# Loading w3 in two awaited halves, and running the last matmuls in four column tiles with four evacuating copies

## Chip, cores, metric

The kernel runs on 1 core of a Trainium2 chip. The metric is the time of one execution on the device, in microseconds, taken as the median of several runs. A profile is one execution; its span (193.5 us for the kernel before) is counted from the first to the last instruction and is about 1.8 us shorter than the time. All times in profiles below are counted from the span's start.

## The reference, cut to what matters

One decode step of a small transformer block for 8 sequences: a layernorm, attention over a window of 2048 cached keys and values (64 MB of K and V), and then an MLP part. Only the end matters here:

```python
h = x + attention(layernorm(x)) @ wo                 # [8, 512]
# with one token the shifted branch through w1, w2 is zero, so
# B(y) = y + gelu(layernorm(y) @ w3) @ w4, y = layernorm(h)
out = h + B(layernorm(h))                            # w3 [512, 1792], w4 [1792, 512], bf16
```

## The kernel before

All loads go through one DMA queue, in one order; the weights of the last stages come last:

```python
order += [("wo", 0), ("wo", 1), ("w3", 0), ("w4", 0)]
...
elif kind == "w3":
    e.dma_start(w3_sb, B_w3.rearrange("(k p) f -> p k f", k=KC)).then_inc(sem_w3, 16)     # 1792 KB
else:                                        # w4 in three pieces: 1024, 512 and 256 KB
    ...                                      # W4_CUT = [0, 8, 12, 14], of FC = 14 row chunks
    e.dma_start(w4_dst[:, c0:c1, :], w4_rows[:, c0:c1, :]).then_inc(sem_w4[i], 16)
```

The end of the compute, cut. `uT` is the normalized input, transposed; `hpx_hi`, `hpx_lo` are the residual in two bf16 parts. In `pe_fin` the 8 columns of a chunk of `gT` are the stationary operand and w4 streams; with NQ = 2 the output columns 0 to 255 go to PSUM partitions 0 to 7 and columns 256 to 511 to partitions 32 to 39, that is to two column tiles of the array.

```python
NQ = 2
DQ = D // NQ
def pe_h3(e):                                # L757: 14 x 4 matmuls of 8 columns
    e.wait_ge(sem_w3, 16)
    e.wait_ge(sem_dveP, DVEP_U)
    for fc in range(FC):
        for kc in range(KC): ...             # w3 chunk stationary, uT moving
def act_gelu(e): ...                         # L768: gT <- misc
def pe_fin(e):
    ...                                      # L778: residual, 8 matmuls of 128 columns
    e.wait_ge(sem_actP, ACTP_G)
    for fc in range(FC):                     # L787
        if fc in W4_CUT:
            e.wait_ge(sem_w4[W4_CUT.index(fc)], 16)
        for j in range(NQ):
            ins = e.matmul(fin_ps[32 * j:32 * j + B, :], gT[:, fc * B:(fc + 1) * B],
                           w4_sb[:, fc, j * DQ:(j + 1) * DQ], ..., tile_position=(0, 32 * j))
def dve_final(e):                            # L797
    e.tensor_copy(out_sb[:, 0:DQ], fin_ps[0:B, :])
def act_final(e):                            # L804
    e.activation(out_sb[:, DQ:D], fin_ps[32:32 + B, :], ACT.Copy)
```

Of the kernel before, what the change touches and what calls it, by code (L numbers as in the profile page):

```python
# [7 lines left out]
ACT = mybir.ActivationFunctionType  # L8
# [3 lines left out]
B = 8  # L12
D = 512
# [8 lines left out]
FC = F // 128  # L22
KC = D // 128
# [14 lines left out]
def bass_sequential_preLN__sliding_block_cached__mixer_s_mlp__decode_kernel(  # L38
# [24 lines left out]
    with es:  # L63
        sb = lambda shape, dtype, name: es.enter_context(nc.sbuf_tensor(name, shape, dtype))
        ps_t = lambda shape, dtype, name: es.enter_context(nc.psum_tensor(name, shape, dtype))
        S = lambda name: es.enter_context(nc.semaphore(name))
# [62 lines left out]
        hpx_lo = sb([128, KB], dt.bfloat16, "hpx_lo")  # L129
        uT = sb([128, KB], dt.bfloat16, "uT")  # L130
        gT = sb([128, FC * B], dt.bfloat16, "gT")
        NQ = 2
        DQ = D // NQ
        out_sb = xln_b

# [4 lines left out]
        misc = ps_t([128, 512], dt.float32, "misc")  # L140
# [3 lines left out]
        H3 = slice(384, 384 + FC * B)  # L144
# [1 line left out]
        sem_slot = [S(f"sem_slot{i}") for i in range(NS)]  # L146
        sem_x = S("sem_x")
        sem_wq = S("sem_wq")
        sem_w3 = S("sem_w3")
        sem_w4 = [S(f"sem_w4_{i}") for i in range(3)]  # L150
        sem_wo = [S(f"sem_wo{i}") for i in range(4)]
        sem_out = S("sem_out")
# [27 lines left out]
        sem_dveP = S("sem_dveP")  # L180
        sem_actP = S("sem_actP")
# [53 lines left out]
        w3_sb = slots[:, place[("w3", 0)][0], 0:KC * F].rearrange("p (k f) -> p k f", k=KC)  # L235
# [11 lines left out]
        def sp_prog(e):  # L247
            e.dma_start(wq_sb, A_wq.rearrange("(p k) n -> p (k n)", k=KC)).then_inc(sem_wq, 16)  # L248

            def free_slot(n):  # L250
                if n >= NS:
                    kind, t = order[n - NS]
                    if kind == "k":
                        e.wait_ge(sem_Thi, NT * (t + 1))
                    else:
                        e.wait_ge(sem_PV, t + 1)
                elif n >= NS - 2:
                    e.wait_ge(sem_dveP, DVEP_QBLK)

            for n, (kind, t) in enumerate(order):  # L260
                free_slot(n)
                slot = n % NS
                dst = slots[:, slot, :]
                if kind in "kv":
                    b, gq = divmod(t, 2)
                    cache = A_k_cache if kind == "k" else A_v_cache
                    src = cache[b, GL * gq:GL * (gq + 1), W0:SK, :].rearrange("g (p c) d -> p g (c d)", c=C)
                    e.dma_start(dst, src).then_inc(sem_slot[slot], 16)  # L268
                elif kind == "wo":
                    for i in range(len(WO_CUT) - 1):  # L270
                        h0, h1 = WO_CUT[i], WO_CUT[i + 1]
                        if h0 // WO_HALF == t:
                            f0 = (h0 % WO_HALF) * D
                            e.dma_start(dst[:, f0:f0 + (h1 - h0) * D],
                                        A_wo.rearrange("(p j) n -> p (j n)", j=NJ)[:, h0 * D:h1 * D]).then_inc(sem_wo[i], 16)
                elif kind == "w3":
                    e.dma_start(w3_sb, B_w3.rearrange("(k p) f -> p k f", k=KC)).then_inc(sem_w3, 16)
                else:
                    w4_rows = B_w4.rearrange("(c p j) n -> p c (j n)", p=128, j=2)
                    w4_dst = w4_sb.rearrange("p (c j) n -> p c (j n)", j=2)  # L280
                    for i in range(len(W4_CUT) - 1):
                        c0, c1 = W4_CUT[i] // 2, W4_CUT[i + 1] // 2
                        e.dma_start(w4_dst[:, c0:c1, :], w4_rows[:, c0:c1, :]).then_inc(sem_w4[i], 16)
            e.wait_ge(sem_dveP, DVEP_OUT_READY)
            e.wait_ge(sem_actP, ACTP_OUT_READY)
            e.dma_start(out.rearrange("b s d -> (b s) d"), out_sb[:, :]).then_inc(sem_out, 16)
            e.wait_ge(sem_out, 16)
# [386 lines left out]
        fin_ps = b6[:, 0:DQ]  # L674
# [73 lines left out]
        PEP_H3 = ev_pe.next()  # L748

        def pe_h3(e):  # L750
            e.wait_ge(sem_w3, 16)
            e.wait_ge(sem_dveP, DVEP_U)
            ins = None
            for fc in range(FC):
                c, j = divmod(fc, 2)
                for kc in range(KC):
                    ins = e.matmul(misc[:, H3.start + fc * B:H3.start + (fc + 1) * B],  # L757
                                   w3_sb[:, kc, c * 256:(c + 1) * 256].rearrange("p (q j) -> p j q", j=2)[:, j, :],
                                   uT[:, kc * B:(kc + 1) * B],
                                   start=(kc == 0), stop=(kc == KC - 1))  # L760
            ins.then_inc(sem_peP, 1)
        PE.append(pe_h3)

        ACTP_G = ev_act.next()
# [8 lines left out]
        def pe_fin(e):  # L773
            e.wait_ge(sem_dveP, DVEP_RES)
            for half in (hpx_hi, hpx_lo):
                for k in range(KC):
                    j, kk = divmod(k, KC // NQ)
                    e.matmul(fin_ps[32 * j:32 * j + B, kk * 128:(kk + 1) * 128], half[:, k * B:(k + 1) * B],  # L778
# [4 lines left out]
# [5 lines that stand above are left out]
# [6 lines left out]

        def dve_final(e):
            e.wait_ge(sem_peP, PEP_FIN)
            e.tensor_copy(out_sb[:, 0:DQ], fin_ps[0:B, :]).then_inc(sem_dveP, 1)  # L797
        DV.append(dve_final)

        ACTP_OUT_READY = ev_act.next()  # L800

        def act_final(e):
            e.wait_ge(sem_peP, PEP_FIN)
            e.activation(out_sb[:, DQ:D], fin_ps[32:32 + B, :], ACT.Copy).then_inc(sem_actP, 1)  # L804
        AC.append(act_final)

        with nc.Block() as block:
            block.gpsimd(pool_prog)
            block.sync(sp_prog)

            @block.tensor
            def _(e):
                for f in PE:
                    f(e)

            @block.scalar
            def _(e):
                for f in AC:
                    f(e)

            @block.vector
            def _(e):
                for f in DV:
                    f(e)
# [28 lines left out]
```

## Time and profile before

| what | before |
|---|---|
| time, median (range) | 195.37 us (195.1 to 195.4, 3 runs) |
| DMA engines busy, slices 2 to 38 of 40 | 9 tenths or more |
| HBM read | 79.18 MB, 409 GB/s over the span |
| w3 / first piece of w4 lands (all of it has arrived) | 185.6 / 188.2 us |
| last matmul ends | 191.3 us |
| output DMA issued, span ends | 191.8, 193.5 us |

The page's activity rows, two of them (busy tenths in 40 equal slices of the span; the granted clock of TensorE in tenths of full speed):

```profile
PEclk9999999859999999699999998899999999998557
DMA  6999999999999999999999999999999999999981
```

The DMA row is full until the last two slices: the kernel is bound by its loads, and only what comes behind the last loads can be shortened. The next fence is the end of the chain of waits, in order of time (start, length, what):

```profile
150.91 37.24 DMA slots<-in_B_w_dram
188.16 0.14 issue
188.29 3.03 PE b L787 x28
191.32 0.02 issue
191.34 0.41 DVE xln_b L797
```

From 150.91 to 188.16 us everything that ended last was waiting for a load of B's weights, here the first piece of w4; then 28 matmuls, then one copy on VectorE beside one on ScalarE. The timeline of the same stretch shows what stood ready and what did not (start, length, engine, line, operation, count; in brackets the idle time before it and what ended that):

```profile
184.31 0.19 DVE L734 SCALAR_TENSOR_TENSOR uT<-hm,r 128x32 bf16<-128x32 f32 x1
185.66 1.66 PE L757 MATMUL misc<-uT,slots 128*128 128x8 bf16 x56 [2.62 <-DMA slots<-in_B_w_dram]
187.35 0.26 ACT L768 ACTIVATE gT<-misc 128x112 bf16<-128x112 f32 x1 [1.61 <-PE misc L757]
188.29 3.01 PE L787 MATMUL b<-slots,gT 128*8 128x256 bf16 x28 [0.45 <-DMA slots<-in_B_w_dram]
191.34 0.37 ACT L804 ACTIVATE xln_b<-b 8x256 bf16<-8x256 f32 x1 [3.73 <-PE b L787]
191.34 0.41 DVE L797 CAST xln_b<-b 8x256 bf16<-8x256 f32 x1 [5.84 <-PE b L787]
```

uT was ready at 184.50 and the w3 matmuls waited for w3 until 185.66. That looks like lost time. But the gelu ended at 187.61, and the last matmuls still had to wait for w4, until 188.29: the w3 stage had 0.55 us to spare. The windows of this stretch (start:end, length, busy us of PE, PEld, DVE, ACT, POOL with counts, granted clock, DMA share, GB/s) show two more things:

```profile
186.00:186.50 0.50, 0.50 (x25) 0.50 (x22) 0.00 (x0) 0.00 (x0) 0.00 (x0) 0.50 1.02 397
187.00:187.50 0.50, 0.50 (x18) 0.48 (x17) 0.00 (x0) 0.15 (x1) 0.00 (x0) 0.50 0.59 225
189.00:189.50 0.50, 0.50 (x8) 0.29 (x6) 0.00 (x0) 0.00 (x0) 0.00 (x0) 0.50 0.58 201
191.00:191.50 0.50, 0.30 (x6) 0.00 (x0) 0.15 (x1) 0.16 (x1) 0.00 (x0) 0.97 0.00 0
```

The clock stands at half in the whole tail (in the trace of before it rises at 191.03, and the last two matmuls took 280 and 277 ns in place of 417). And from about 186.7 us on the DMA share falls to 0.59.

### The profile page before, as it was taken

The page shows a single profiled execution, that of the slowest core. Times are in us where ns is not written, and L with a number is a line of the kernel's source. Part 1 is how long each engine was busy: PE and PEld are TensorE (multiplying, and loading weights), DVE is VectorE, ACT ScalarE, POOL GpSimd, SP SyncE. Part 2 cuts the span into 40 slices and gives each one's busy share as a digit, 9 for nine tenths or more (in the row PEclk, how much of TensorE's full clock was granted, in tenths as well). Part 3 has the DMA queues.
Part 4 walks back from the last instruction along what each step waited for, and adds up shares of the span by engine and source line. Part 5 has one row for each costly group of instructions (what it writes and reads, how often), then busy time and mean ns, then how long its engine had stood idle before and what let it go on. Part 6 is the DMA issues. An engine that isn't in the chain of part 4 may idle for free.

```text
span 193.5 us, 4989 instructions
## 1 busy us (share of the span) xinstructions
PE 152.7 (79%) x2088; PEld 106.2 (55%) x2088; DVE 106.4 (55%) x277; ACT 90.3 (47%) x109; POOL 4.7 (2%) x14
## 2 busy tenths in 40 slices
PE   2037999399979993999799766999699999765555
PEld 0037878286647562766475444756566684435443
DVE  7811447343787375447763672558647877673220
ACT  3110577924494465245944382348445965400040
POOL 8000000000000000000000000000000000000000
PEclk9999999859999999699999998899999999998557
DMA  6999999999999999999999999999999999999981
GB/s 225 427 433 433 427 430 430 430 425 433 430 433 423 425 427 433 433 423 433 427 433 422 427 427 430 433 423 433 433 427 427 430 435 427 433 422 402 412 331 40
DMA packets 6853, 79.50 MB, mean 411 GB/s; under 512 B 672, under 2 KB 688, under 8 KB 2352
## 3 DMA queue, kind: packets, MB, share of 16 engines
q1 hardware_dynamic: 6816, 79.18, 96.6%
q8 instruction: 17, 0.28, 0.5%
q14 instruction: 4, 0.03, 0.0%
q10 hardware_dynamic: 16, 0.01, 0.0%
HBM read 79.18 MB, written 0.01 MB: 409 GB/s over the span
## 4 chain that ended last, share of the span: by engine, by line
DMA 80%; PE 17%; SPq 1%; issue 0%; DVE 0%
DMA slots<-in_A_k_cache_dram 60%; DMA slots<-in_B_w_dram 19%; PE kT_ps L430 9%; PE S_ps L462 2%; PE misc L551 2%; PE b L787 2%; PE b L551 2%; SPq L268 1%; PE misc L513 0%; PE misc L573 0%; DVE xln_b L797 0%; SPq L248 0%; PE b L573 0%
## 5 line engine op out<-in xcount | busy, mean ns | idle before, releaser
L441 ACT ACTIVATE kT_sb<-kT_ps 128x1024 bf16<-128x1024 bf16 x64 | 65.3, 1023 | 68.9 <-PE kT_ps L430 68.9
L430 PE MATMUL kT_ps<-perm_b,slots 128*128 128x128 bf16 x1024 | 72.2, 228 | 17.4 <-DMA slots<-in_A_k_cache_dram 17.0
L430 PEld LDWEIGHTS kT_ps<-perm_b,slots 128*128 128x128 bf16 x1024 | 62.4, 103 | 34.9 <-DMA slots<-in_A_k_cache_dram 20.5
L447 DVE COPY kT_sb<-kT_ps 128x1024 bf16<-128x1024 bf16 x64 | 43.7, 685 | 54.0 <-PE kT_ps L430 53.9
L462 PE MATMUL S_ps<-kT_sb,qstrip 128*32 128x512 bf16 x256 | 24.8, 399 | 0.3 <-DVE kT_sb L447 0.3
L496 ACT ACTIVATE P_sb<-S_ps,mtile 128x1024 bf16<-128x1024 f32 x16 | 17.8, 1113 | 2.4 <-DVE mtile L485 2.4
L551 PE MATMUL misc<-slots,pT_sb 128*64 128x512 bf16 x128 | 16.7, 384 | 1.1 <-DVE mrl L519 1.1
L551 PE MATMUL b<-slots,pT_sb 128*64 128x512 bf16 x128 | 16.5, 384 | 0.0
L530 DVE TENSOR_TENSOR pT_sb<-kT_ps,maskT 128x1024 bf16<-128x1024 bf16 x16 | 10.6, 688 | 2.8 <-PE kT_ps L430 2.5
L430 PE MATMUL kT_ps<-ident_b,P_sb 128*128 128x128 bf16 x128 | 11.0, 254 | 0.0
L430 PEld LDWEIGHTS kT_ps<-ident_b,P_sb 128*128 128x128 bf16 x128 | 9.4, 116 | 2.3 <-issue 1.5
L551 PEld LDWEIGHTS misc<-slots,pT_sb 128*64 128x64 bf16 x128 | 6.1, 109 | 7.9 <-issue 3.0
L462 PEld LDWEIGHTS S_ps<-kT_sb,qstrip 128*32 128x32 bf16 x256 | 5.9, 93 | 6.8 <-ACT kT_sb L441 0.8
L551 PEld LDWEIGHTS b<-slots,pT_sb 128*64 128x64 bf16 x128 | 6.1, 109 | 6.1 <-issue 1.5
L567 DVE SCALAR_TENSOR_TENSOR o_sum<-b,mrl,o_sum 128x128 f32<-128x128 f32 x24 | 8.4, 351 | 0.8
L567 DVE SCALAR_TENSOR_TENSOR o_sum<-misc,mrl,o_sum 128x128 f32<-128x128 f32 x24 | 8.4, 350 | 0.8
L679 ACT ACTIVATE std<-var,eps_t 128x8 f32<-128x8 f32 x1 | 0.3, 300 | 17.1 <-DVE var L730 17.1
L363 PE MATMUL b<-ident_b,xln_b 8*128 8x8 bf16 x4 | 0.3, 174 | 7.9 <-DVE xln_b L340 7.9
L474 DVE TENSOR_REDUCE mtile<-S_ps 128x1 f32<-128x512 f32 x8 | 5.4, 681 | 0.6 <-PE S_ps L462 0.6
L363 PEld LDWEIGHTS b<-ident_b,xln_b 8*128 8x128 bf16 x4 | 0.2, 114 | 8.8 <-DVE xln_b L340 8.8
L383 PE MATMUL S_ps<-xlnT,slots 128*128 128x8 bf16 x128 | 3.6, 168 | 1.6 <-DMA slots<-in_A_wq_dram 1.6
L697 PE MATMUL S_ps<-opl,slots 128*128 128x8 bf16 x128 | 4.0, 168 | 0.8 <-DMA slots<-in_A_wo_dram 0.8
(96 smaller groups left out, 92.8 us busy)
## 6 DMA issues: line engine op xcount, KB each, us to landing
slots<-in_A_k_cache_dram SPq DMA_DIRECT2D x16, 2048.0 KB, 40.4
slots<-in_A_v_cache_dram SPq DMA_DIRECT2D x16, 2048.0 KB, 38.6
slots<-in_A_wq_dram SPq DMA_DIRECT2D x1, 4096.0 KB, 12.3
slots<-in_A_wo_dram SPq DMA_DIRECT2D x1, 2048.0 KB, 41.0
slots<-in_B_w_dram SPq DMA_DIRECT2D x1, 1792.0 KB, 39.5
slots<-in_A_wo_dram SPq DMA_DIRECT2D x1, 1024.0 KB, 34.0
slots<-in_A_wo_dram SPq DMA_DIRECT2D x2, 512.0 KB, 35.2
slots<-in_B_w_dram SPq DMA_DIRECT2D x1, 1024.0 KB, 37.2
```

The lines of the kernel that those rows point to most:

```text
L383: ins = e.matmul(S_ps[:, 0, h * B:(h + 1) * B], wq_v[:, kc, h * DH:(h + 1) * DH], xlnT[:, kc * B:(kc + 1) * B], start=(kc == 0), stop=(kc ...
L430: ins = e.matmul(kT_ps[n % 2][:, c * 128:(c + 1) * 128], src[:, c * 128:(c + 1) * 128], unit[:, :], is_transpose=True)
L441: e.activation(kT_sb[:, i % NKT, 0:W // 2], kT_ps[step_of[("k", i)] % 2][:, 0:W // 2], ACT.Copy).then_inc(sem_Elo, 1)
L447: e.tensor_copy(kT_sb[:, i % NKT, W // 2:W], kT_ps[step_of[("k", i)] % 2][:, W // 2:W]).then_inc(sem_Ehi, 1)
L462: ins = e.matmul(S_ps[32 * gl:32 * (gl + 1), b % 2, :], qstrip[:, b, GL * gq + gl, o:o + 32], kv[:, gl, :, :], start=(gq == 0 and qi == 0) ...
L474: ins = e.tensor_reduce(mtile[:, 2, 0:1], S_ps[:, j, :], AX.X, ALU.max)
L496: e.activation(P_sb[:, half * W // 2:(half + 1) * W // 2].rearrange("r (k g) -> r k g", g=GL), s_rep, ACT.Exp, bias=mtile[:, j, 0:1], scal ...
L530: e.tensor_tensor(pT_sb[:, :, half * hc:(half + 1) * hc, :].rearrange("p a c (g x) -> p (c g) a x", g=GL), kT_ps[n % 2][:, half * W // 2:( ...
L551: ins = e.matmul(pv_ps[gq][64 * a:64 * (a + 1), :].rearrange("p (q d) -> p q d", d=DH), pT_sb[:, gq, cc, :], vq[:, cc, :, :], start=(cc < ...
L567: ins = e.scalar_tensor_tensor(o_sum[:, gq, :], pv_ps[gq][:, q * DH:(q + 1) * DH], w[:, q:q + 1], o_sum[:, gq, :], ALU.mult, ALU.add)
L697: ins = e.matmul(hT_ps[:, k * B:(k + 1) * B], wo_at(h)[:, k * 128:(k + 1) * 128], opl[:, h, :], start=False, stop=(h == NJ - 1), skip_grou ...
L787: ins = e.matmul(fin_ps[32 * j:32 * j + B, :], gT[:, fc * B:(fc + 1) * B], w4_sb[:, fc, j * DQ:(j + 1) * DQ], start=False, stop=(fc == FC ...
```

## The change

Its intent: start the w3 matmuls as soon as the first half of w3 is there, and halve the time of the last matmuls by running four column tiles of 128 output columns side by side in place of two of 256. The evacuation, which is the copying of the result out of PSUM, then takes two copies on each engine. NQ = 4 also spreads the 8 residual matmuls over four tiles. In the w3 matmuls the first pass leaves all 14 sums open until the second pass adds the other two chunks of rows, and the `start` flag now stands on the very first matmul alone.

```diff
-        NQ = 2
+        NQ = 4
-        sem_w3 = S("sem_w3")
+        sem_w3 = [S(f"sem_w3_{i}") for i in range(2)]
...
-                    e.dma_start(w3_sb, B_w3.rearrange("(k p) f -> p k f", k=KC)).then_inc(sem_w3, 16)
+                    for i in range(2):
+                        k0, k1 = i * KC // 2, (i + 1) * KC // 2
+                        e.dma_start(w3_sb[:, k0:k1, :],
+                                    B_w3.rearrange("(k p) f -> p k f", k=KC)[:, k0:k1, :]).then_inc(sem_w3[i], 16)
...
-            e.wait_ge(sem_w3, 16)
             e.wait_ge(sem_dveP, DVEP_U)
-            for fc in range(FC):
-                for kc in range(KC): ...
-                                   start=(kc == 0), stop=(kc == KC - 1))
+            for half in range(2):
+                e.wait_ge(sem_w3[half], 16)
+                for fc in range(FC):
+                    for kc in range(half * KC // 2, (half + 1) * KC // 2): ...
+                                       start=(kc == 0 and fc == 0), stop=(kc == KC - 1), skip_group_check=True)
...
-            e.tensor_copy(out_sb[:, 0:DQ], fin_ps[0:B, :]).then_inc(sem_dveP, 1)
+            for j in range(NQ // 2):
+                ins = e.tensor_copy(out_sb[:, j * DQ:(j + 1) * DQ], fin_ps[32 * j:32 * j + B, :])
+            ins.then_inc(sem_dveP, 1)
...                                                                # and the same on ScalarE for j = 2, 3
```

More of the change, by code (lines that the diff above doesn't have):

```diff
@@ L750, in pe_h3 @@
         def pe_h3(e):
-            e.wait_ge(sem_w3, 16)
             e.wait_ge(sem_dveP, DVEP_U)
             ins = None
-            for fc in range(FC):
-                c, j = divmod(fc, 2)
-                for kc in range(KC):
-                    ins = e.matmul(misc[:, H3.start + fc * B:H3.start + (fc + 1) * B],
-                                   w3_sb[:, kc, c * 256:(c + 1) * 256].rearrange("p (q j) -> p j q", j=2)[:, j, :],
-                                   uT[:, kc * B:(kc + 1) * B],
-                                   start=(kc == 0), stop=(kc == KC - 1))
+            for half in range(2):
+                e.wait_ge(sem_w3[half], 16)
+                for fc in range(FC):
+                    c, j = divmod(fc, 2)
+                    for kc in range(half * KC // 2, (half + 1) * KC // 2):
+                        ins = e.matmul(misc[:, H3.start + fc * B:H3.start + (fc + 1) * B],
+                                       w3_sb[:, kc, c * 256:(c + 1) * 256].rearrange("p (q j) -> p j q", j=2)[:, j, :],
+                                       uT[:, kc * B:(kc + 1) * B],
+                                       start=(kc == 0 and fc == 0), stop=(kc == KC - 1), skip_group_check=True)
             ins.then_inc(sem_peP, 1)
@@ L803, in act_final @@
             e.wait_ge(sem_peP, PEP_FIN)
-            e.activation(out_sb[:, DQ:D], fin_ps[32:32 + B, :], ACT.Copy).then_inc(sem_actP, 1)
+            for j in range(NQ // 2, NQ):
+                ins = e.activation(out_sb[:, j * DQ:(j + 1) * DQ], fin_ps[32 * j:32 * j + B, :], ACT.Copy)
+            ins.then_inc(sem_actP, 1)
         AC.append(act_final)
```

## The prediction

> **What bounds the kernel now.** DMA: the activity rows show the DMA engines at 9 tenths or more from slice 2 to slice 37, and the chain of waits gives 80% of the 193.5 us span to DMA. So only what follows the last weights can be saved. The chain in order of time ends: B weights in flight until 188.16 us; the 28 last matmuls 188.29 to 191.32; the evacuation 191.34 to 191.75; the output DMA to 193.5.
>
> The last landings, from the DMA issues with their times to landing: w3 issued 146.1 + 39.5 = 185.6; w4 in three pieces 150.9 + 37.2 = 188.1, 167.9 + 21.5 = 189.4, 177.5 + 12.5 = 190.0. The w3 matmuls run 185.66 to 187.2 (56 starts about 28 ns apart), the gelu ends at 187.61, and then PE waits, for w4 piece 0.
>
> **Half A, w3 in two halves.** The first half should land about 2.1 us before the second (896 KB at the 390 to 430 GB/s of these windows), near 183.4. uT is ready at 184.50 (timeline), so 28 matmuls run at about 184.6 to 185.4, the other 28 from 185.65 to about 186.4. The gelu then ends near 186.9 instead of 187.6. But w4 piece 0 lands only at 188.16, and the gelu already had 0.55 us of slack before it. I expect these 0.7 us to become wait: worth 0 by itself.
>
> **Half B, four column tiles.** The 28 matmuls of 256 columns start in pairs, 6 ns apart, a pair every 0.2135 us, at a granted clock of 0.50 (windows, 188 to 191). The Trainium skill ("TensorE: Matmul & The Clock Gate", back-to-back issue gap) gives N / 1.2 ns for a cold array: 213 for 256 columns, which this trace agrees with; two column tiles therefore already run side by side. With four tiles of 128 columns it gives 107 ns per group of four; the residual matmuls here (128 columns) follow each other in one tile every 106 ns. 56 weight loads and matmuls at the 28 ns per pair of the w3 stage give about the same: 14 groups x 107 to 112 ns = 1.5 to 1.6 us in place of 3.0.
>
> Not all of that is kept, because w4 pieces 1 and 2 now become waits: piece 0's eight groups 188.3 to 189.2, wait until 189.4; four groups to 189.95; wait until 190.05; two groups and the drain, end near 190.65. Before: 191.30. PE gain about 0.65 us.
>
> **Evacuation.** ACT took 374 ns and DVE 413 ns for 8x256, side by side. Now each makes two copies of 128. A DVE cast of 128 columns takes 279 ns here; two, overlapped, I estimate at 0.47 us, so 0.05 to 0.1 us more. The output DMA keeps its 1.75 us.
>
> **Sum.** -0.65 + 0.08 = about -0.6 us: 194.8 us, 8 in 10 between 194.2 and 195.3. Faster by over 2%: 0.01; within 2%: 0.97; slower: 0.02.
>
> **What would show it.** The wait of the w3 matmuls split in two, the second ending near 185.6; the gelu near 186.9 and a wait of over 1 us for w4 after it; last matmuls starting in fours about 0.11 us apart, with gaps near 189.3 and 190.0; last matmul end near 190.6, after which two copies per engine take about 0.47 us.
>
> **What would make it wrong.** The split w3 or the added instructions shifting the w4 landings (a few tenths of a us either way, the same size as the gain); groups of four not overlapping (56 x 107 ns = 6 us, 3 us slower); copies that do not overlap (+0.15 us); a clock that stays low does not matter much[...].

## The result, and the profile after

The changed kernel took 194.88 us (194.62 to 194.94, 4 runs) beside 195.38 us for the kernel before (195.1 to 195.61, 4 runs). A ratio is the mean time of one kernel's runs over that of the other's runs of the same rounds, so it is not quite the ratio of the medians: 0.998, 95% interval 0.9964 to 0.9995. It is 0.5 us less by the medians. In five more rounds (below) it was 0.68 us less, ratio 0.9964 (0.9951 to 0.9976). The prediction of 194.8 us, 194.2 to 195.3, holds. All outputs are right.

The timeline after, the lines that answer to those of before:

```profile
184.47 0.91 PE L761 MATMUL misc<-uT,slots 128*128 128x8 bf16 x28 [1.52 <-DVE uT L737]
185.60 0.91 PE L761 MATMUL misc<-uT,slots 128*128 128x8 bf16 x28 [0.22 <-DMA slots<-in_B_w_dram]
186.55 0.26 ACT L772 ACTIVATE gT<-misc 128x112 bf16<-128x112 f32 x1 [0.89 <-PE misc L761]
188.19 1.03 PE L791 MATMUL b<-slots,gT 128*8 128x128 bf16 x32 [1.37 <-DMA slots<-in_B_w_dram]
190.47 0.56 ACT L811 ACTIVATE xln_b<-b 8x128 bf16<-8x128 f32 x2 [3.65 <-PE b L791]
190.47 0.57 DVE L802 CAST xln_b<-b 8x128 bf16<-8x128 f32 x2 [5.05 <-PE b L791]
191.11 0.37 SPq L289 DMA_DIRECT2D out_dram<-xln_b  x1
```

The first half of the w3 matmuls now starts with uT, the gelu ends 0.8 us earlier (186.81), and all of that becomes a wait: PE sits idle 1.37 us, until the first piece of w4. The last matmuls come in three runs, 32, 16 and 8, and the chain of waits shows why:

```profile
167.88 21.47 DMA slots<-in_B_w_dram
189.35 0.04 issue
189.39 0.60 PE b L791 x16
189.99 0.04 issue
190.03 0.41 PE b L791 x8
190.44 0.02 issue
190.47 0.28 DVE xln_b L802
190.74 0.30 DVEq L815
```

The long wait now ends at 189.35, with w4's second piece, no longer with its first; the third lands at 189.98. The last matmul ends at 190.41, in place of 191.30, 0.89 us earlier. The evacuation (from the first copy's start to the output DMA's issue) takes 0.64 us in place of 0.46. The output DMA is issued at 191.11 in place of 191.81: 0.70 us earlier, and 0.70 us is also what the span lost (193.54 to 192.84). Each of these is one execution against one. The clock rise in the trace of before flatters before by about 0.14 us: from e1 to e2 below, which have no such rise before the matmuls end, the last matmul's end moves from 191.53 to 190.53, 1.0 us, and the output DMA's issue 0.80 us.

### The profile page after: what moved, and what is told of

Same layout as the page of the kernel before. It is cut to its first block, busy times and chain, and to the rows that moved or that the text cites. A ratio compares the mean times of both kernels' runs of the same rounds, so it can differ in the third digit from the quotient of the medians. Undisturbed runs are those within 1.5% of the kernel's fastest.

```text
span 192.8 us, 5048 instructions
## 1 busy us (share of the span) xinstructions
PE 151.7 (79%) x2116; PEld 105.5 (55%) x2116; DVE 106.4 (55%) x278; ACT 90.6 (47%) x110; POOL 4.8 (2%) x14
## 4 chain that ended last, share of the span: by engine, by line
DMA 76%; PE 18%; SPq 4%; DVE 1%; issue 0%; DVEq 0%
DMA slots<-in_A_k_cache_dram 65%; DMA slots<-in_B_w_dram 11%; PE kT_ps L433 10%; PE S_ps L465 2%; PE misc L554 2%; SPq L268 2%; PE b L554 2%; SPq L286 2%; PE b L791 1%; DVE kT_sb L450 0%; PE misc L516 0%; PE b L576 0%; PE misc L576 0%; SPq L248 0%; DVEq L815 0%
## 5 line engine op out<-in xcount | busy, mean ns | idle before, releaser
L576 PE MATMUL b<-o_sum,hsel 128*16 128x128 f32 x16 | 3.8, 330 | 1.4 <-DVE o_sum L570 1.4
```

The costliest lines, as they stand in the source:

```text
L576: e.matmul(pv_ps[v % 2][0:GL * R, OT], hsel[:, :], o_sum[:, v % 2, :], start=True, stop=True).then_inc(sem_oTm, 1)
```

## The experiments

Four theories were to be told apart. Mine: the landing of w4 sets the tail, so the w3 halves are worth nothing, and the tiles are worth only the part that does not turn into waits for w4's second and third pieces. The rivals: the halves do part of the work; the tiles cannot be fed faster than they were; and, for the two copies that took 0.57 us where I had expected 0.47, either a cost of changing the PSUM rows or plain lack of overlap.

### Each half of the change alone

e1: the changed kernel with

```diff
-        NQ = 4
+        NQ = 2
```

> The change's first half alone (w3 in two halves, two column tiles as before). Theory (the w4 landing near 188.1 us decides): 0 us; 195.4 +- 0.1; gelu ends near 186.8 instead of 187.6, then PE waits over 1.2 us for w4; last matmul still ends near 191.3. Rival (the halves give part of the gain): 0.2 to 0.5 us less, last matmuls starting earlier than 188.2.

Measured: 195.54 us beside 195.56, ratio 1.0001 (0.9987 to 1.0014). The timeline of e1:

```profile
186.78 0.26 ACT L772 ACTIVATE gT<-misc 128x112 bf16<-128x112 f32 x1 [1.20 <-PE misc L761]
188.38 3.15 PE L791 MATMUL b<-slots,gT 128*8 128x256 bf16 x28 [1.11 <-DMA slots<-in_B_w_dram]
```

The gelu ended at 187.04, the matmuls still waited for w4 until 188.38 and ended at 191.53. The halves alone are worth nothing, although they do exactly what they were meant to do.

e2: the kernel before with NQ = 4 and the four copies; w3 loaded and awaited whole:

```diff
-        NQ = 2
+        NQ = 4
-            e.tensor_copy(out_sb[:, 0:DQ], fin_ps[0:B, :]).then_inc(sem_dveP, 1)
+            for j in range(NQ // 2): ...          # as in the change; the same on ScalarE
```

> The change's second half alone (four column tiles and four copies, w3 as one load). Theory: the whole gain, 194.9 +- 0.15, last matmul ends near 190.4, copies as in the changed kernel. Rival: clearly slower than the changed kernel of the same rounds (by 0.2 us or more).

The timeline of e2:

```profile
188.35 2.17 PE L787 MATMUL b<-slots,gT 128*8 128x128 bf16 x56 [0.59 <-DMA slots<-in_B_w_dram]
```

e3: the changed kernel once more, no edit.

> The changed kernel once more, in the same rounds, to size the gain more tightly: the traces' shift of the output DMA's issue (191.81 to 191.11) says 0.7 us, the first timed runs say 0.5; between 194.6 and 195.0.

| run, same rounds | median us | ratio to before | 95% interval |
|---|---|---|---|
| before | 195.56 | | |
| e1, w3 halves alone | 195.54 | 1.0001 | 0.9987 to 1.0014 |
| e2, tiles and copies alone | 194.73 | 0.9960 | 0.9947 to 0.9972 |
| e3, the whole change | 194.88 | 0.9964 | 0.9951 to 0.9976 |

The tiles alone give all of the gain, 0.83 us here (194.82 beside 195.49 in a later set, r2 below: 0.67 us); the whole change gave 0.68. The intervals of e2 and e3 overlap. The first half of the change can be left out.

### The landing order turned round

If the halves and the tiles are worth more than they show because w4 lands last, then both must show their full worth when w3 lands last. That takes one edit, made to four kernels:

```diff
-        order += [("wo", 0), ("wo", 1), ("w3", 0), ("w4", 0)]
+        order += [("wo", 0), ("wo", 1), ("w4", 0), ("w3", 0)]
```

f1 is the kernel before with it, f2 is e1 with it, f3 is e2 with it, f4 the changed kernel with it.

> The kernel before with w4 loaded ahead of w3, so that w3 is what lands last (near 190.1 us) and no wait for w4 remains behind it. It is the base for the three runs beside it. Chain after the landing: w3 matmuls 1.66, gelu 0.3, last matmuls 3.1, evacuation 0.41: about 3.8 us above the kernel before, 199.4.

> The same with w3 in two halves. Theory (the halves do shorten the path to the gelu, and were worth nothing only because w4 landed later): 0.7 to 0.8 us below the base run. Rival (halves give nothing by themselves, e.g. because the second load's landing or the split loop costs as much): within 0.2 us of the base run.

> The same base with four column tiles and four copies. Theory (about 0.5 us of the tiles' gain went into waits for w4 pieces 1 and 2): last matmuls of 1.5 + 0.3 us without a gap in place of 3.1, copies 0.16 us longer, so 1.1 to 1.3 us below the base run, against 0.7 to 0.8 in the real order. Rival (groups of four cannot be fed faster than they were): 0.7 to 0.8 us here too.

> Both halves of the change in this order. Theory: the two gains add, 1.8 to 2.1 us below the base run. Rival: no more than the tiles alone.

| run, same rounds | median us | against f1 | the same part in the real order |
|---|---|---|---|
| f1, before | 199.25 | | |
| f2, w3 halves | 198.56 | -0.69 | -0.02 (e1) |
| f3, tiles and copies | 197.97 | -1.28 | -0.83 (e2), -0.67 (r2) |
| f4, both | 197.17 | -2.08 | -0.68 (e3) |

Lines of the chain of waits of f1, then of f2, then of f3:

```profile
190.12 1.65 PE misc L757 x56
192.30 3.00 PE b L787 x28
```

```profile
190.07 0.91 PE misc L761 x28
191.50 3.00 PE b L791 x28
```

```profile
190.10 1.66 PE misc L757 x56
192.11 1.69 PE b L787 x56
```

And one line of the timeline of f3:

```profile
192.11 1.67 PE L787 MATMUL b<-slots,gT 128*8 128x128 bf16 x56
```

With nothing left to wait for, the 56 narrow matmuls run without a gap in 1.67 us from the first start to the last end, where the 28 wide ones took 3.16 (192.13 to 195.29 in the timeline of f1; the chain counts only the last 3.00 of it). In e2, with the waits for w4's second and third pieces, the same 56 took 2.17: 0.50 us more. The Trainium skill, "TensorE: Matmul & The Clock Gate", section "Back-to-back issue gap", gives N / 1.2 ns as the gap between single matmuls on a cold array. That is 107 ns for 128 columns, taken here as an estimate for a step of four tiles side by side; the trace of the changed kernel agrees, with 0.107 us from group to group of four at a granted clock of 0.50, after a first step of 0.06 (its 32 matmuls: 0.06 + 6 x 0.107 + 0.31 for the last one's own length = 1.01 of the 1.03 us shown). What sets the step is not told apart: the w3 matmuls follow each other every 27 ns, and four times that is 107 ns too. The halves, worth nothing before, are worth 0.69 us here. The two add up: 0.69 + 1.28 = 1.97, measured 2.08. So the rivals fall: neither part of the change is idle by itself, and the tiles can be fed. What they lost in the real order is the difference, about 0.5 us of the tiles' gain and all of the halves', and the wait that took it is the one for w4. The order itself is a bad one for this kernel (f1 is 3.6 us slower than the kernel before, 195.64 in these rounds), since more work stands behind the last landing.

### The two copies that did not overlap

I had expected two copies of 128 columns to take 0.47 us. In the changed kernel VectorE's second copy began 14 ns after the first had ended, ScalarE's 12 ns. The Trainium skill, "VectorE: DVE Perf Modes", section "Two Vector instructions with no wait between them", has a rule for that: an instruction whose input starts in another group of 32 partitions than the last instruction's input from the same memory is held until all earlier ones have finished. With four tiles the copies of one engine read PSUM rows 0 and 32 (VectorE) or 64 and 96 (ScalarE). e4 makes the same number of copies of the same size, but in the kernel before, where both copies of an engine read the same rows:

```diff
-            e.tensor_copy(out_sb[:, 0:DQ], fin_ps[0:B, :]).then_inc(sem_dveP, 1)
+            for j in range(2):
+                ins = e.tensor_copy(out_sb[:, j * 128:(j + 1) * 128], fin_ps[0:B, j * 128:(j + 1) * 128])
+            ins.then_inc(sem_dveP, 1)
...                                                # and the same on ScalarE, rows 32 to 39
```

> The kernel before with only its evacuation cut into four copies of 128 columns, so both copies of an engine read the same 32-row group of PSUM. Theory (the second copy in the changed kernel is held because its input starts in another 32-row group than the one before it): here DVE's two copies overlap, second start 60 to 150 ns before the first's end, pair about 0.45 us. Rival (two copies never overlap here, e.g. because both engines read one bank): gap of 10 to 15 ns and a pair of 0.56 us as in the changed kernel. Time 195.4 to 195.6.

Measured: 195.63 us beside 195.56 (ratio 0.9999, 0.9985 to 1.0013). The timeline of e4:

```profile
191.60 0.43 ACT L807 ACTIVATE xln_b<-b 8x128 bf16<-8x128 f32 x2 [3.88 <-PE b L787]
191.60 0.48 DVE L798 CAST xln_b<-b 8x128 bf16<-8x128 f32 x2 [5.96 <-PE b L787]
```

The pairs take 0.48 and 0.43 us in place of 0.57 and 0.56, with copies of nearly the same length in both kernels (278 and 269 ns on VectorE against 278 and 282 ns after; 268 and 253 ns on ScalarE against 270 and 273 ns). VectorE's second copy starts 70 ns before the first ends, ScalarE's 92 ns. So the change of PSUM rows, not the number of copies, takes the overlap away, as the page says for VectorE. (The columns read differ too: 0 to 127 in both copies of the changed kernel, 0 to 127 and 128 to 255 in e4. That was not separated.) It costs about 0.1 us on each engine here. The second copy by itself costs only about 0.07 us (0.48 against 0.41).

### An attempt at something better

Since the slowest DMA engines set the end, and the DMA share is 0.59 from 186.7 us on, I tried to find the engines that finish early and to give them more of w4. The Trainium skill, "DMA: Bandwidth & Descriptors", section "Why a DMA increments its semaphore by 16 and not by 1", says that a load is split over the largest k of at most 16 engines that divides its rows, on the lowest-numbered ones. So I put eight tiny loads of 14, 12, ... 1 rows ahead of w4 in e2:

```diff
+                    for n_, rows in enumerate((14, 12, 10, 8, 6, 4, 2, 1)):
+                        e.dma_start(dst[0:rows, FC * D + 128 * n_:FC * D + 128 * n_ + 98 + 2 * rows],
+                                    B_w1[0:rows, 0:98 + 2 * rows]).then_inc(sem_junk, 16)
```

Its first build asked for more SBUF than was left and did not build; the second used unused bytes of w4's slot.

> The tiles-alone kernel with eight tiny loads (14, 12, 10, 8, 6, 4, 2 and 1 rows of an unused input, each of its own size) put ahead of w4, to see in the packet times which of the 16 DMA engines are ahead when the last weights come. From 186.5 us on the DMA share is 0.59, so six or seven engines have finished some 3 us before the others. If the engines that are ahead are those that take the small loads (the first ones), the markers' packets start about 2.5 us before the others' and the last piece of w4 can be moved to them; if they are spread, nothing simple is to be had. Time not of interest, 194.7 to 195.5.

> The tiles-alone kernel with eight tiny loads (14, 12, 10, 8, 6, 4, 2 and 1 rows of an unused input, each of its own size, into unused bytes) put ahead of w4, to see in the packet times which of the 16 DMA engines are ahead when the last weights come. From 186.5 us on the DMA share is 0.59, so six or seven engines have finished some 3 us before the others. If the engines that are ahead are those that take the small loads (the first ones), the markers' packets start about 2.5 us before the others' and the last piece of w4 can be moved to them; if they are spread, nothing simple is to be had. Time not of interest, 194.7 to 195.8.

It is one run (195.17 us beside 195.48, state unknown), used for its packet times alone. The starts of the packets of the 14-, 2- and 1-row loads, read from the packed trace since no view lists single packets, in us:

```
14 rows: 182.05 182.05 182.11 182.11 182.13 182.82 184.44 184.84 184.86 184.88 185.02 185.02 185.32 185.61
 2 rows: 182.17 182.94
 1 row:  182.19
```

Each load was one packet per row, as k = rows wants. Six of the fourteen engines were 2.8 to 3.6 us ahead of the latest. Those that carried the 2-row load, the first two if the page's numbering holds, were among them; the others that were ahead were mixed with late ones. One candidate for the lag was not looked at: the trace of m2 also holds 17 instruction loads of 16 KB, each 0.88 to 1.19 us long and 15 of them before the markers. If they fell on some of the engines only, that may have put these behind; which engines they took is not in the trace. r1 then loaded the last two of w4's seven row blocks in parts of 80, 14 and 34 rows (16, 14 and 2 engines), on top of e2; r2 is e2 again, as its base:

```diff
-                        e.dma_start(w4_dst[:, c0:c1, :], w4_rows[:, c0:c1, :]).then_inc(sem_w4[i], 16)
+                        ...                        # piece 1's first block whole, as before
+                        for p0, p1 in [(0, 128)] if i == 0 else [(0, 80), (80, 94), (94, 128)]:
+                            e.dma_start(w4_dst[p0:p1, c0:c1, :], w4_rows[p0:p1, c0:c1, :]).then_inc(sem_w4[i], 16)
```

> Four column tiles alone (w3 in one load), and the last 2 of w4's 7 row blocks each loaded in three parts of 80, 14 and 34 rows, which go to 16, 14 and 2 DMA engines: in the marker run the first two engines were about 3 us ahead, the others in part late. Per engine, the twelve middle ones move 4 packets of 80 ns less. Theory (the slowest DMA engine sets the end): w4's last piece lands 0.2 to 0.3 us earlier and the run is 0.2 to 0.3 us below the tiles-alone kernel of the same rounds. Rival (the engines that are ahead differ from run to run, or total bandwidth sets the end): same or slower.

> The tiles-alone kernel once more, as the base of the run beside it and to size it again: 0.6 to 0.8 us below the kernel before.

Measured: r1 195.62 us, r2 194.82, before 195.49. r1 is a miss, 0.8 us slower than its base. The timelines of r1, then of r2:

```profile
189.35 1.90 PE L791 MATMUL b<-slots,gT 128*8 128x128 bf16 x56 [1.57 <-DMA slots<-in_B_w_dram]
```

```profile
188.36 2.16 PE L787 MATMUL b<-slots,gT 128*8 128x128 bf16 x56 [0.69 <-DMA slots<-in_B_w_dram]
```

In r1 w4's first piece, which was not touched, landed 1.0 us later (189.22 against 188.22 in r2). From 186.0 to 188.5 us the mean time of a 2 KB packet was 97 to 136 ns, by half microseconds, where r2 had 84 ns throughout. So the uneven cut made the packets themselves slower, which cost more than the shift could save; why it did was not found out. No run beat both kernels by more than noise; e2, the simpler one, equals the change.

## Why the prediction was right, point by point

- **"So only what follows the last weights can be saved."** Right. The whole change moved the time by 0.5 to 0.7 us; turning round which weight lands last moved it by 3.6 us.
- **"I expect these 0.7 us to become wait: worth 0 by itself."** Right, and shown: the first half of w3 landed at 183.37 as expected (183.4); e1 gave a ratio of 1.0001, with the gelu at 187.04 and a wait for w4 after it. That it was the landing of w4 that made it worthless is shown by f2, where the same half gives 0.69 us.
- **"14 groups x 107 to 112 ns".** Right: 0.107 us from group to group, and 1.67 us for all 56 in f3, the last one's own length included.
- **"Not all of that is kept, because w4 pieces 1 and 2 now become waits".** Right in kind. After piece 0's groups the next start is 189.39, after piece 1's 190.03. Without those waits the tiles gave 1.28 us, with them 0.67 to 0.83.
- **"end near 190.65", "PE gain about 0.65 us".** Mis-sized. The last matmul ended at 190.41, a gain of 0.89. Two terms: I took 0.14 us from a landing to the first matmul, as at piece 0 before (188.16 to 188.29), but at pieces 1 and 2 it took 0.04 (189.35 to 189.39, 189.99 to 190.03); and the first step between two groups was 0.06 us, not 0.107. The landing itself was also 0.07 us earlier in this run. The 191.30 that I measured from was early as well, by the 0.14 us of the clock rise; from e1 to e2 the gain is 1.0.
- **"two, overlapped, I estimate at 0.47 us".** Wrong as a step: they did not overlap. It took 0.57 us, and e4 showed that two copies do take 0.48 when they read the same rows. So the evacuation cost 0.16 us more, not 0.05 to 0.1.
- **The sum.** Expected -0.65 + 0.08 = -0.6 (rounded); the traces show -0.89 for the matmuls and +0.19 from there to the output DMA's issue, -0.70 together, and the timed runs -0.50 and -0.68. The two wrong sizes partly cancelled, so the total was closer than its terms, which is luck.
- **The risk named first, that the split w3 would shift the w4 landings,** did not come: they landed at 188.06, 189.35 and 189.98 in place of 188.16, 189.41 and 190.05; in e1 they came 0.09 to 0.15 us later (188.25, 189.56, 190.19), in e2, where w3 is not split, 0.05 to 0.06 later, and e1's time equals that of before. So this is the spread between executions.
- **"a clock that stays low does not matter much"** Not tested: every trace has half clock in this stage but for the very end of before, and the last two matmuls there, 256 columns wide, did get shorter (280 and 277 ns in place of 417).

## What to carry to other kernels

Before a wait is shortened, look at which landing ends last behind it: here a wait of 1.1 us for w3 could be cut by most of a microsecond for nothing, because w4 landed 2.5 us after w3 and had to be waited for anyway, while a change behind the last landing paid at once, until it met the next piece's landing. When matmuls with few stationary columns run in column tiles, more tiles can pay even at the low clock, as here; but plan the evacuation with them, since here each engine that went from one group of 32 PSUM rows to another lost the overlap of its copies.

## What the Trainium skill lacked or had wrong

- "ScalarE: Activation LUTs" says that back-to-back ACTIVATEs overlap by about 93 ns. e4 agrees (92 ns), but when the second one read PSUM from the next group of 32 rows there was none: 0.56 us for a pair in place of 0.43, with a gap of 12 ns. The page has no such rule for ScalarE; "VectorE: DVE Perf Modes" has it for VectorE (0.57 in place of 0.48 us).
- "TensorEngine Tiling (Array Packing)" warns that the evacuation may become the bottleneck, but it does not say that copies over more groups of 32 rows lose their overlap, though its tables put the tiles there; here that cost about 0.1 us of a gain of 0.7.
- No page that I found gives a figure for how far the 16 DMA engines of one queue drift apart over a kernel: six of the fourteen that could be told apart were 2.8 to 3.6 us ahead of the latest when the last weights began (m2), though the large loads all have 128 rows; why is open. Cutting the last loads unevenly made 2 KB packets take up to 136 ns in place of 84 (r1); why is open.
